# A gated mix of a spectral filter and a dense Mish layer: gate weights as one row, w1 in three other pieces, four tiles transposed by DMA, a narrower last output, and a new order

## The chip, the cores and the metric

The kernel runs on one core of a Trainium2 chip. The metric is the device time of one execution in microseconds. A profile shows one execution: the engines are TensorE (PE in the profile, its weight loads PEld), VectorE (DVE), ScalarE (ACT), GpSimd (POOL) and SyncE (SP). SP and ACT also issue DMAs (SPq and ACTq in the profile).

## The reference

```python
# A_x: 1 x 2048 x 512; w_r, w_i: 2048 x 257; w1: 512 x 1792; w2: 1792 x 512; all bf16
g = sigmoid((x * gate_w).sum(-1, keepdims=True))           # one gate for each of 2048 rows
a = irfft2(rfft2(x) * (w_r + 1j * w_i))                    # spectral filter over rows and columns
h = x @ w1 + b1
b = (h * tanh(softplus(h))) @ w2                           # dense layer with Mish
return g * a + (1 - g) * b
```

Both branches take the same x.

## The kernel before, in words

All 2048 rows are held as 16 tiles of 128 rows (row 16p + t stands on partition p of tile t). Two chains of work share TensorE.

The dense branch: each tile is transposed on TensorE (`tr0` to `tr15`, L544: four 128-wide transposes) and copied from PSUM to `xT` (`evx`, L475). For each of four chunks of 512 rows and each of 14 slices of w1 there is one product `m{chunk}_{slice}` (L788: four 512-wide matmuls) and one Mish activation `h{chunk}_{slice}` on ScalarE (L792). An output tile then is `n{tile}_0` (L815: 14 matmuls, 512 wide).

The spectral branch is a two-dimensional Fourier transform made of small matrix products, each group being four 128-wide matmuls: `p` over the partitions (L567), `d` over the columns (L581, with the constants `FD`, loaded by `cFD`), a shuffle by DMA through SBUF (`sh`), `t` (L666, constants `M`, loaded by `ldM`), the filter on VectorE (`p2`, `p1`, `ad`, L679 to L687, with the weights copied into place by `wrm`, `wim`, `win` and duplicated by the DMAs `wrn`), an edge correction (`e1`, `xp`, `ead`, `e2`, `e3`), and then the way back: `it` (L740), a DMA shuffle `hx`, `id` (L764), `ec` and `ey` on VectorE and ScalarE, and `ip` (L799). Results of `p`, `d`, `t`, `it` are evicted from PSUM 1024 elements wide by `ep`, `ed`, `et`, `eit` (L475) on ScalarE or VectorE.

The gate: `gt` (L589, VectorE, one for each tile) multiplies a tile by the gate weights and sums; `ez`, `ez1`, `omg`, `gc` make g and 1 - g. The gate weights must stand on all 128 partitions (`gwr`); the DMA `gw` reads the one row 128 times. An output tile is scaled and added by `o` and `s` (L804, L805, L809) and leaves by `out` DMAs.

The order is written out by hand as one string (`ORDER`): each token names a task, its engine and its PSUM banks or scratch buffers. Each engine runs its tasks strictly in that order, and the semaphores follow from the data. A wait on one engine therefore holds everything behind it on that engine. A DMA stands in the order of the engine that issues it. The filter products cannot start before all copies of w_r and w_i into place that they need, the activations `h2` wait for the `sh` DMAs and `h3` for all weight copies, because their outputs take over that memory. `warm` and the fillers `fl0`, `fl1`, `fl2` (products with ones, 14 and 3, 8, 5 of them) keep TensorE at work in the beginning. `tab` is a one-element Mish activation at the head of ScalarE's list, which brings the activation table.

Of the kernel before, what the change touches and what calls it, by code (L numbers as in the profile page):

```python
# [306 lines left out]
h0_3:act evx5:act tr6:pe:4 evx6:dve tr4:pe:6 tr7:pe:7 evx7:act cFD:sp evx4:dve
p4:pe:2 p5:pe p6:pe:0 p7:pe h0_5:act ep6:act m1_4:pe:7 m1_3:pe:6 h1_3:act
gt0:dve ep4:dve gt1:dve gt2:dve m1_2:pe:2 gt3:dve h1_2:act h1_4:act bf8_0:dve
bf8_1:dve gt4:dve m0_11:pe:3 h0_11:act m1_8:pe:6 h1_8:act tr11:pe:7 evx11:act m0_7:pe:2  # L310
h0_7:act m1_10:pe:6 h1_10:act bf12_1:dve tr9:pe:7 evx9:dve p8:pe:0 p9:pe ep8:act
m0_9:pe:2 tr8:pe:3 p10:pe:4 bf12_0:dve p11:pe p12:pe:0 p13:pe p14:pe:6 p15:pe
h0_9:act ep10:act ep12:act gt5:dve ep14:dve m1_6:pe:2 h1_6:act m0_10:pe:4 h0_10:act
d6:pe:0 evx8:dve gt6:dve gt7:dve gt8:dve d7:pe tr10:pe:2 d4:pe:6 d5:pe
tr12:pe:3 m1_12:pe:4 evx12:dve ed3:act gt9:dve m0_13:pe:5 ed2:act tr15:pe:3 d2:pe:0
d3:pe h1_12:act h0_13:act ed1:act evx15:dve gt10:dve gt11:dve evx10:act d0:pe:6
d1:pe d14:pe:4 d15:pe m1_11:pe:3 m0_8:pe:0 ed0:act ed7:act m1_0:pe:2 tr14:pe:1
h0_8:act h1_11:act wi0s1:sp wi0s2:sp evx14:act wr0s1:sp wr0s0:sp wr1s1:sp wr1s0:sp
wrm001:dve wrm010:dve gt12:dve gt13:dve gt14:dve wrm100:dve d8:pe:4 d9:pe m0_6:pe:6
m1_9:pe:3 tr13:pe:7 gt15:dve wip0:pool wip1:pool ed4:act h1_0:act h0_6:act evx13:dve  # L320
m0_4:pe:1 d12:pe:4 d13:pe m1_1:pe:2 h0_4:act h1_9:act ed6:act h1_1:act d10:pe:0
d11:pe m1_5:pe:3 ed5:act m1_7:pe:4 wi0s0:sp m2_8:pe:2 m0_12:pe:5 m3_11:pe:0 wi1s1:sp
sh0_3:sp sh0_0:sp wim011:dve sh0_2:sp h1_5:act ldM0:sp wim111:dve wrm000:dve wim100:dve
wrm110:dve wim101:dve zcl:dve sh0_1:sp wim110:dve m3_0:pe:3 wrm011:dve t1_0:pe:6 wrm101:dve
wrm111:act h1_7:act t1_1:pe wim000:dve wim001:dve wim010:dve m3_10:pe:4 et1:act win0:dve
h3_0:act h0_12:act m3_2:pe:1 t0_0:pe:6 t0_1:pe et0:dve wic0:dve win1:dve m3_9:pe:3
m1_13:pe:5 wiz0:dve p20_0:dve:0 p21_0:dve:1 h3_2:act h3_11:act h3_10:act ez:pool ldM1:sp
t3_0:pe:0 t3_1:pe sh1_0:sp sh1_2:sp sh1_3:sp sh1_1:sp h1_13:act et3:act m2_10:pe:4
h2_10:act h2_8:act m2_9:pe:5 h2_9:act h3_9:act m2_12:pe:0 t2_0:pe:6 t2_1:pe m2_6:pe:1
m2_4:pe:3 wrn01:sp wrn00:sp et2:act p20_1:dve p21_1:dve p23_0:dve:2 p23_1:dve h2_4:act  # L330
m3_4:pe:6 ldM3:sp t6_0:pe:4 wrc0:dve wrz0:dve p1_3:dve ez1:dve omg:dve ad_3:dve
p1_1:dve t6_1:pe h2_12:act et6:act p1_0:dve wic1:dve t7_0:pe:2 t7_1:pe m2_7:pe:0
et7:act h2_7:act m2_11:pe:7 ldM2:sp wrn10:sp t5_0:pe:4 wiz1:pool ad_0:dve ad_1:dve
t5_1:pe m2_2:pe:2 h2_2:act et5:act wrn11:sp wrc1:dve m3_3:pe:0 m3_6:pe:3 m2_3:pe:2
t4_0:pe:4 t4_1:pe p27_0:dve:0 wrz1:dve p26_0:dve:1 h3_6:act h3_3:act et4:act m3_7:pe:3
m2_1:pe:0 h2_1:act h2_6:act h2_11:act m3_8:pe:4 m3_12:pe:5 m2_13:pe:1 m3_1:pe:7 p22_0:dve:2
p27_1:dve p22_1:dve p1_7:dve p26_1:dve p1_6:dve ad_7:dve h3_12:act h2_13:act p1_2:dve
p25_0:dve:0 ad_6:dve w2_9:sp w2_4:sp w2_0:sp p24_0:dve:1 n5_0:pe:5 h3_8:act h3_7:act
h3_1:act h3_4:act p25_1:dve p24_1:dve ad_2:dve p1_5:dve ad_5:dve edge:sp ldG0:sp
p1_4:dve ad_4:dve o5_0:dve n6_0:pe:3 o6_0:act h2_3:act e1:pe:5 gc:dve xp20:dve:0  # L340
xp21:dve xp1:dve:1 rft:sp ldG3:sp ead:dve:2 m2_5:pe:6 m2_0:pe:7 h2_5:act h2_0:act
inv:sp ldG1:sp e2:pe:2 m3_13:pe:3 e3:dve ldG2:sp it1_0:pe:0 it1_1:pe eit1:dve
it5_0:pe:4 it5_1:pe h3_13:act eit5:act m3_5:pe:7 h3_5:act it2_0:pe:2 it2_1:pe it7_0:pe:0
eit2:act it3_0:pe:4 it3_1:pe it7_1:pe eit7:act eit3:act n4_0:pe:7 it0_0:pe:0 it4_0:pe:2
it0_1:pe it6_0:pe:4 it6_1:pe it4_1:pe eit6:act eit4:act eit0:dve hx8_0:act hx4_1:act
hx8_1:act o4_0:act hx0_0:act n0_0:pe:6 n2_0:pe:2 n3_0:pe:7 id10:pe:0 id11:pe id8:pe:4
hx4_0:act ec10:dve:0 ey10_1:dve ey10_0:dve id9:pe ec8:act:1 hx12_0:act o2_0:act o0_0:act
ey8_0:dve ey8_1:dve n1_0:pe:3 id6:pe:0 ip9:pe:6 o1_0:act o9:act id4:pe:4 ip10:pe:2
id5:pe id7:pe ec6:act:0 ip8:pe:3 ip11:pe:6 hx0_1:sp hx12_1:sp o3_0:dve o11:dve
ec4:act:1 o8:act n7_0:pe:7 ey6_1:dve ey6_0:dve o10:act ip6:pe:6 ip7:pe:0 ey4_0:dve  # L350
id2:pe:2 ey4_1:dve ip4:pe:1 id0:pe:4 id1:pe id3:pe ec0:act:0 o7_0:act s6:dve
ec2:act:1 s4:dve ey0_0:dve n11_0:pe:6 ey0_1:dve s7:dve ey2_1:dve id12:pe:0 ip0:pe:7
ip5:pe:4 id13:pe n10_0:pe:5 s11_0:dve s5:dve s0:dve ey2_0:dve ip3:pe:4 id14:pe:2
id15:pe ip1:pe:7 ec12:act:0 out5:act out7:act ec14:act:1 ey12_1:dve ey12_0:dve ip12:pe:6
ip2:pe:0 n8_0:pe:1 s1:dve ey14_0:dve ey14_1:dve ip13:pe:7 ip15:pe:2 n9_0:pe:3 s3:dve
s8_0:dve s10_0:dve ip14:pe:1 out11:sp out1:sp s2:dve o12:dve n12_0:pe:6 s12_0:dve
n13_0:pe:0 o13:dve s13_0:dve s9_0:dve o14:dve out13:act o15:act out3:act out9:sp
n15_256:pe:7 n14_0:pe:6 s14_0:dve out14:act s15_256:dve out15_256:sp n15_0:pe:1 s15_0:dve out15_0:act
"""


def _build(nc, A_x, A_w_r, A_w_i, B_x, B_w1, B_b1, B_w2, gate_w, out, XTP=16, LATE=8, NWARM=14,
           W1P=((0, 2), (2, 6), (6, 14)), XP=((0, 2), (2, 4), (4, 8), (8, 12), (12, 16)), SH=2):
# [7 lines left out]
    G = _Graph()  # L371
    es = ExitStack()
    with es:
# [100 lines left out]
        def evac(name, o, i, n, reads, writes, cls, engs=("act", "dve"), deps=()):  # L474
            fns = dict(dve=lambda e: e.tensor_copy(out=o(), in_=i()), act=lambda e: e.activation(o(), i(), AF.Copy))  # L475
# [410 lines left out]
```

## Time and profile before

| | us |
|---|---|
| runs | 135.01, 133.9, 134.84 (median 134.84) |
| the profiled execution: its time | 134.83 |
| its span, from the first instruction to the last | 133.2 |
| TensorE busy | 127.2 (95%) |
| VectorE busy | 87.9 (66%) |
| ScalarE busy | 77.4 (58%) |
| GpSimd busy | 5.4 (4%) |

The granted TensorE clock is 1.0 throughout. A row such as "80.36 3.02 PE ps L815 x14" of the chain of waits says: from 80.36 us on, 3.02 us of the chain are 14 instructions of line 815 on TensorE that write `ps`. In a row of the groups stand the line, engine, operation, output and inputs, shapes and count, then busy time and the mean of one in ns, then the idle time ahead of them and what ended it. In the rows of the DMA issues the last number is the time from issue to landing in us.

### The profile page before, as it was taken

How to read it: one execution, taken by the hardware profiler on the slowest of the kernel's cores; microseconds unless marked ns; L12 is line 12 of the kernel's file. 1: busy time of each engine (PE TensorE's matmuls, PEld its weight loads, DVE VectorE, ACT ScalarE, POOL GpSimd, SP SyncE). 2: the span in 40 equal slices, each digit the busy share in tenths (PEclk: the TensorE clock that was granted, in tenths of full speed). 3: DMA queues.
4: the chain of work that ended last, by engine and by line, in shares of the span. 5: the costliest groups of instructions: out<-in, count | busy, mean ns of one | idle time of the engine just before them, and what ended most of it. 6: DMA issues, size and time to landing. Idle time of an engine off the chain costs nothing.

```text
span 133.2 us, 2246 instructions
## 1 busy us (share of the span) xinstructions
PE 127.2 (95%) x901; PEld 71.5 (54%) x901; DVE 87.9 (66%) x162; ACT 77.4 (58%) x110; POOL 5.4 (4%) x13
## 2 busy tenths in 40 slices
...
GB/s 100 145 351 407 307 205 170 172 56 0 245 270 199 219 229 238 220 259 359 348 316 1 0 0 5 0 241 310 74 9 0 0 58 99 0 162 0 0 236 79
DMA packets 12533, 20.28 MB, mean 152 GB/s; under 512 B 1324, under 2 KB 6956, under 8 KB 12460
## 3 DMA queue, kind: packets, MB, share of 16 engines
...
q8 instruction: 7, 0.11, 0.4%
q14 instruction: 2, 0.02, 0.0%
...
## 4 chain that ended last, share of the span: by engine, by line
PE 58%; DVE 30%; DMA 6%; issue 4%; SPq 1%; DVEq 0%
PE ps L815 32%; PE ps L788 14%; DVE tmp L679 7%; DMA w_sb<-in_B_w_dram 6%; DVE rC L684 4%; DVE rC L687 4%; PE ps L740 3%; PE ps L764 3%; PE ps L799 3%; PE ps L567 2%; DVE w_sb L589 2%; DVE rW L630 2%; DVE rA L630 2%; DVE rA L640 2%; PE ps L544 2%
## 5 line engine op out<-in xcount | busy, mean ns | idle before, releaser
L788 PE MATMUL ps<-rX,w_sb 128*128 128x512 bf16 x224 | 51.9, 379 | 1.7 <-DMA w_sb<-in_B_w_dram 1.7
L788 PEld LDWEIGHTS ps<-rX,w_sb 128*128 128x128 bf16 x224 | 20.8, 98 | 23.3 <-issue 1.9
L815 PE MATMUL ps<-w_sb,hs 128*128 128x512 bf16 x112 | 25.0, 379 | 0.0
L792 ACT ACTIVATE hs<-ps,b1f 128x512 bf16<-128x512 f32 x28 | 18.5, 696 | 3.4 <-PE ps L788 3.2
L815 PEld LDWEIGHTS ps<-w_sb,hs 128*128 128x128 bf16 x112 | 10.8, 98 | 12.4
L475 ACT ACTIVATE rC<-ps 128x1024 bf16<-128x1024 f32 x13 | 13.2, 1031 | 1.2 <-PE ps L567 0.7
L815 PE MATMUL ps<-w_sb,rD 128*128 128x512 bf16 x56 | 12.7, 379 | 0.0
L557 DVE TENSOR_TENSOR rB<-rA 128x1024 bf16<-128x1024 bf16 (+1 forms) x10 | 5.5, 580 | 11.0 <-DMA rA<-in_A_x_dram 11.0
L815 PE MATMUL ps<-w_sb,rS 128*128 128x512 bf16 (+1 forms) x70 | 12.3, 336 | 0.0
L809 DVE SCALAR_TENSOR_TENSOR rX<-ps,omg,rX 128x512 bf16<-128x512 f32 (+1 forms) x9 | 5.9, 689 | 9.3 <-PE ps L815 9.3
L475 ACT ACTIVATE tmp<-ps 128x512 f32<-128x512 f32 x7 | 4.1, 597 | 13.4 <-PE ps L764 13.3
L589 DVE SCALAR_TENSOR_TENSOR w_sb<-rA,w_sb 128x512 bf16<-128x512 bf16 x16 | 11.0, 687 | 0.3
L792 ACT ACTIVATE rD<-ps,b1f 128x512 bf16<-128x512 f32 x14 | 9.1, 698 | 3.1 <-PE ps L788 3.1
L679 DVE TENSOR_TENSOR tmp<-rC,rA 64x1024 bf16<-64x1024 bf16 x16 | 10.6, 686 | 0.4
L804 ACT ACTIVATE rX<-ps,gcol 128x512 bf16<-128x512 f32 x4 | 2.6, 690 | 14.0 <-DVE rX L809 14.0
L774 DVE TENSOR_TENSOR rA<-tmp,ps 128x512 bf16<-128x512 f32 x16 | 10.0, 679 | 0.4 <-ACT tmp L475 0.4
L815 PEld LDWEIGHTS ps<-w_sb,rS 128*128 128x128 bf16 x70 | 6.8, 98 | 5.5
L792 ACT ACTIVATE rS<-ps,b1f 128x512 bf16<-128x512 f32 x14 | 9.0, 696 | 0.7 <-PE ps L788 0.3
L815 PEld LDWEIGHTS ps<-w_sb,rD 128*128 128x128 bf16 x56 | 5.4, 98 | 6.1
L804 ACT ACTIVATE rX<-ps,omg 128x512 bf16<-128x512 f32 x6 | 4.0, 685 | 7.4 <-PE ps L815 5.1
L475 ACT ACTIVATE rD<-ps 128x1024 bf16<-128x1024 f32 x8 | 8.0, 1035 | 0.0
L475 ACT ACTIVATE rF<-ps 128x1024 bf16<-128x1024 f32 x6 | 5.8, 1029 | 2.2 <-PE ps L740 2.2
...
## 6 DMA issues: line engine op xcount, KB each, us to landing
rE<-rD SPq DMA_DIRECT2D x8, 256.0 KB, 3.6
...
rC<-rF ACTq DMA_DIRECT2D x6, 256.0 KB, 3.4
w_sb<-in_B_w_dram SPq DMA_DIRECT2D x2, 640.0 KB, 11.4
...
```

The source lines that it names most:

```text
L475: fns = dict(dve=lambda e: e.tensor_copy(out=o(), in_=i()), act=lambda e: e.activation(o(), i(), AF.Copy))
L557: return e.tensor_tensor(out=xu[:, a:b_, uv, :], in0=x_sb[:, a:b_, 0:256], in1=x_sb[:, a:b_, 256:512], op=ALU.add if uv == 0 else ALU.subt ...
L589: t_gt.append(dve(f"gt{t}", "gate", "stt", 512, lambda e, t=t: e.scalar_tensor_tensor(out=junk, in0=x_sb[:, t, :], scalar=1.0, in1=gwr, op ...
L630: return e.tensor_copy(out=o_, in_=i_)
L679: return e.tensor_tensor(out=zv(z)[lo], in0=Y[hi, f0:f0 + 8, :], in1=Wi[hi, f0:f0 + 8, 0:128], op=ALU.mult)
L684: return e.tensor_tensor(out=Y[:, f0:f0 + 8, :], in0=Y[:, f0:f0 + 8, :], in1=Wr[:, f0:f0 + 8, 0:128], op=ALU.mult)
L774: return e.tensor_tensor(out=yb[:, t:t + 2, 256 * h:256 * h + 256].rearrange("p t (i e) -> p t i e", e=2), in0=t4(z), in1=o4(bank(b, 1)), ...
L788: ins = e.matmul(bank(b), w1_sb[:, dt_, 128 * ft:128 * (ft + 1)], xT[:, c, dt_, :, :], start=(dt_ == 0), stop=(dt_ == 3))
L792: G.add(f"h{c}_{ft}", "mish", dict(act=lambda e, c=c, ft=ft, b=b: e.activation(hs[c][:, ft, :], bank(b), AF.Mish, bias=b1f[:, ft:ft + 1])) ...
L804: f_a = lambda e: e.activation(o_()[0], o_()[1], AF.Copy, scale=o_()[2])
L809: dve(name, "fin", "psums", hi - lo, lambda e: e.scalar_tensor_tensor(out=bs[:, t, lo:hi], in0=bank(b)[:, 0:hi - lo], scalar=col[:, t:t + ...
L815: ins = e.matmul(bank(b)[:, 0:hi - lo], hs[c][:, ft, 128 * tl:128 * (tl + 1)], w2_sb[:, ft, lo:hi], start=(ft == 0), stop=(ft == NFT - 1))
```

## The change

Five edits and a new order:

- The gate weights come as one row of 1 KB (`gwl`, into a free row of SBUF). A product with a row of ones (`gwb`) spreads it over 128 partitions into PSUM, and `gwe` copies it to `gwr`. The 128 KB broadcast `gw` goes.
- w1 comes in pieces of 4, 5 and 5 slices of 128 columns, where it came in pieces of 2, 4 and 8.
- Tiles 12 to 15 are no longer transposed on TensorE; four DMA transposes (`xt12` to `xt15`, on SP) read x again from memory and write `xT`.
- The last output tile is made in 384 and 128 columns, where it was 256 and 256.
- Of the fillers only `fl0` stays.
- The order of all engines is written anew. Among other things: `x8` and `w1_9` are issued by ACT; `tab` moves from the head of ScalarE's list to a place behind `h3_13`; the wide evictions go to other engines (VectorE has `ep2`, `ep6`, `ep10`, `ep14`, `ed0`, `ed6`, `et5`, `et0`, `et1` up to `e1`, where it had `ep4`, `ep14`, `et0`); the filter weights' copy `wrm101` goes to ScalarE; `n2` and `n1` stand ahead of `e1` and `n5` behind it, where `n5` and `n6` stood ahead; all of m but `m2_0` stands ahead of `e1`.

```diff
-FILL = (3, 8, 5, )
+FILL = (3, )
 ORDER = """
-warm:pe:0 wrp0:pool ebase:pool ones:pool wrp1:pool ident:pool cRF:act braw:act x0:sp
-fl0:pe:1 tr0:pe:0 x2:sp w1_0:sp w1_2:sp bf0_0:dve bf0_1:dve bf2_1:dve x4:sp
-tr1:pe:1 gw:act tab:act bf2_0:dve evx1:dve fl1:pe:2 tr2:pe:2 evx0:act tr3:pe:3
-evx2:act tr_b:pe:0 p0:pe:4 p1:pe p2:pe:6 ep0:act evx3:dve ev_b:dve fl2:pe:2
-m0_1:pe:0 m0_0:pe:1 p3:pe w1_6:sp x8:sp x12:sp h0_1:act wi1s0:act wr0s2:sp
...
-n15_256:pe:7 n14_0:pe:6 s14_0:dve out14:act s15_256:dve out15_256:sp n15_0:pe:1 s15_0:dve out15_0:act
+cRF:act wrp1:pool ones:pool ident:pool braw:act x0:sp warm:pe:0 fl0:pe:1 tr0:pe:0
+tr1:pe:1 gwl:act x2:sp w1_0:sp x4:sp x8:act x12:sp w1_4:sp wr0s0:sp
+wi0s2:sp cFD:sp bf0_0:dve bf0_1:dve tr2:pe:2 tr3:pe:3 tr_b:pe:4 gwb:pe:5 w1_9:act
+wr0s2:act evx0:dve bf2_1:dve bf2_0:dve evx1:act p2:pe:0 p3:pe p0:pe:6 p1:pe
+evx2:act evx3:dve ep0:act wr0s1:act m0_1:pe:3 m0_2:pe:2 gwe:dve gt0:dve gt1:dve
+ev_b:dve ep2:dve tr7:pe:4 tr6:pe:5 m0_3:pe:6 tr5:pe:7 h0_2:act h0_1:act evx7:act
+tr4:pe:3 bf4_1:dve bf4_0:dve p6:pe:0 tr8:pe:2 m0_0:pe:4 p7:pe ldM0:act evx6:act
...
+p15:pe evx9:act ep12:act h0_5:act m1_0:pe:0 m0_4:pe:6 h1_0:act h0_4:act ep14:dve
+d14:pe:2 d15:pe d10:pe:0 d0:pe:4 d1:pe ed7:act gt2:dve ed0:dve gt3:dve
...
+m1_11:pe:4 t2_1:pe h1_11:act p23_0:dve:2 p21_1:dve xt13:sp xt14:sp xt12:sp xt15:sp
+m3_0:pe:6 p23_1:dve m3_9:pe:5 m1_13:pe:4 m0_6:pe:2 m3_11:pe:3 wrm111:act h3_9:act et2:act
...
+m3_7:pe:2 tab:act et6:act h3_8:act h1_13:act wrc1:dve p25_0:dve:1 p27_0:dve:0 m2_6:pe:6
...
+p26_0:dve:1 ad_4:dve p27_1:dve p1_7:dve ad_7:dve p26_1:dve p1_6:dve ad_6:dve omg:dve
+o2_0:act o1_0:dve e1:pe:6 xp20:dve:0 xp1:dve:1 xp21:dve ead:dve:2 n5_0:pe:3 o5_0:act
...
+s9_0:dve s8_0:dve out9:sp out13:sp s10_0:dve out11:sp s7:dve out7:act n15_0:pe:6
+s15_0:dve out15_0:act n15_384:pe:5 s15_384:dve out15_384:act
 """
-def _build(..., XTP=16, LATE=8, NWARM=14, W1P=((0, 2), (2, 6), (6, 14)), ...):
+def _build(..., XTP=12, LATE=8, NWARM=14, W1P=((0, 4), (4, 9), (9, 14)), ...):
...
-        dma("gw", gwr, gate_w.unsqueeze(0).to_broadcast([128, 512]), kb=128, writes=["gw"])
+        dma("gwl", junk[0:1, :], gate_w.unsqueeze(0), kb=1, writes=["gwl", "junk"])
...
         for t in range(XTP, NT):
             dma(f"xt{t}", xT[:, t // 4, :, t % 4, :], xv[:, t, :], queue=("sp",), transpose=True, kb=128, writes=[("xT", t)])

+        gb = _Buf("b1")
+        G.add("gwb", "small", dict(pe=lambda e: e.matmul(bank(gb), one[0:1, :], junk[0:1, :], start=True, stop=True)), ("pe", 1, 512), reads=["gwl"], writes=[gb])
+        evac("gwe", lambda: gwr, lambda: bank(gb), 512, [gb], ["gw"], "small")
...
-                for lo, hi in ([(0, 256), (256, 512)] if t == NT - 1 else [(0, 512)]):
+                for lo, hi in ([(0, 384), (384, 512)] if t == NT - 1 else [(0, 512)]):
                     b2 = _Buf("b1")
-                    keys = [("bs", t, h) for h in (0, 1) if lo <= 256 * h < hi]
+                    keys = bsk if t < NT - 1 else bsk[:1] if lo == 0 else bsk[1:]
```

More of the change, by code (lines that the diff above doesn't have):

```diff
@@ L307 @@
[L307 to L356, printed above, removed]
@@ new lines @@
+wi0s2:sp cFD:sp bf0_0:dve bf0_1:dve tr2:pe:2 tr3:pe:3 tr_b:pe:4 gwb:pe:5 w1_9:act
[3 more added lines that the diff above has]
+tr4:pe:3 bf4_1:dve bf4_0:dve p6:pe:0 tr8:pe:2 m0_0:pe:4 p7:pe ldM0:act evx6:act
+h0_3:act ldM2:act h0_0:act wi1s0:act evx4:dve evx5:dve bf8_0:dve evx8:dve bf8_1:dve
+ep6:dve m1_1:pe:5 h1_1:act m1_3:pe:2 h1_3:act p10:pe:6 p11:pe tr11:pe:4 p4:pe:0
@@ new lines @@
+p5:pe ep4:act p8:pe:2 m1_4:pe:5 h1_4:act p9:pe ep8:act bf12_1:dve ep10:dve
+tr9:pe:0 m0_5:pe:1 tr10:pe:5 bf12_0:dve p12:pe:6 p13:pe p14:pe:2 evx10:dve evx11:dve
+p15:pe evx9:act ep12:act h0_5:act m1_0:pe:0 m0_4:pe:6 h1_0:act h0_4:act ep14:dve
+d14:pe:2 d15:pe d10:pe:0 d0:pe:4 d1:pe ed7:act gt2:dve ed0:dve gt3:dve
+d11:pe m2_13:pe:6 wi1s1:act ed5:act d12:pe:2 d13:pe d8:pe:4 m1_6:pe:7 h1_6:act
+ed6:dve gt4:dve gt5:dve d9:pe ed4:act sh1_3:act m0_11:pe:0 m0_9:pe:7 d6:pe:2
+d7:pe ed3:act gt6:dve gt7:dve gt8:dve d4:pe:4 d5:pe m1_5:pe:1 m0_7:pe:2
@@ new lines @@
+m0_8:pe:3 ed2:act h0_11:act h0_8:act gt9:dve wrm000:dve gt10:dve gt11:dve gt12:dve
+gt13:dve h0_7:act m2_12:pe:0 gt14:dve gt15:dve wim101:dve zcl:dve wim100:dve sh1_2:sp
+wi0s0:sp d2:pe:4 wi0s1:sp wim010:dve wim011:dve wrm010:dve wrm001:dve wrm011:dve sh1_0:act
+sh1_1:act wip0:pool h0_9:act wim001:dve d3:pe ed1:act sh0_3:sp m1_8:pe:3 m1_7:pe:2
+m1_12:pe:7 m0_10:pe:4 h1_8:act h1_5:act h0_10:act sh0_2:sp sh0_1:sp h1_12:act m1_10:pe:3
+m1_9:pe:1 h1_7:act h1_9:act h1_10:act m2_2:pe:7 m1_2:pe:2 m0_13:pe:3 h0_13:act h1_2:act
@@ new lines @@
+sh0_0:sp h2_12:act h2_13:act m2_8:pe:1 h2_8:act t5_0:pe:4 t5_1:pe m2_1:pe:3 m2_7:pe:2
+et5:dve wim000:dve h2_1:act h2_7:act h2_2:act t4_0:pe:4 t1_0:pe:0 t4_1:pe m0_12:pe:6
+h0_12:act win0:dve wic0:dve t0_0:pe:2 t0_1:pe et4:act wr1s0:sp ldM1:sp wr1s1:sp
+t1_1:pe m2_5:pe:7 m2_9:pe:6 wrm101:act et0:dve t3_0:pe:2 m2_4:pe:4 h2_4:act h2_9:act
+wip1:pool wrp0:pool wiz0:pool t3_1:pe m2_10:pe:5 et3:act h2_10:act p20_0:dve:0 wim110:dve
+et1:dve wim111:dve p20_1:dve win1:dve wic1:dve wrm100:dve p21_0:dve:1 wrm110:dve t2_0:pe:0
@@ new lines @@
+m1_11:pe:4 t2_1:pe h1_11:act p23_0:dve:2 p21_1:dve xt13:sp xt14:sp xt12:sp xt15:sp
+m3_0:pe:6 p23_1:dve m3_9:pe:5 m1_13:pe:4 m0_6:pe:2 m3_11:pe:3 wrm111:act h3_9:act et2:act
+h3_11:act h0_6:act wrn01:sp wrn00:sp wrc0:dve wrz0:dve p1_3:dve ad_3:dve p1_0:dve
+ad_0:dve p1_1:dve ebase:pool ldM3:sp wrn10:sp wrn11:sp wiz1:pool ez:pool m3_12:pe:5
+w2_9:sp w2_0:sp h2_5:act w2_4:act m2_11:pe:0 t7_0:pe:2 t7_1:pe m3_3:pe:7 et7:act
+h2_11:act h3_0:act h3_3:act m3_13:pe:1 m3_5:pe:2 m3_8:pe:0 m2_3:pe:3 t6_0:pe:6 t6_1:pe
```

26 lines of the change are left out of this document (22 added, 4 removed).

## The prediction

> **What bounds the kernel now.** I read the page's busy rows first, then the chain of waits, then busy time by stretch.
>
> ```profile
> span 133.2 us, 2246 instructions
> PE 127.2 (95%) x901; PEld 71.5 (54%) x901; DVE 87.9 (66%) x162; ACT 77.4 (58%) x110; POOL 5.4 (4%) x13
> ```
>
> ```profile
> 1.71 7.49 DMA w_sb<-in_B_w_dram
> 9.33 1.89 PE ps L788 x8
> ...
> 14.03 0.89 PE ps L544 x16
> ...
> 30.28 0.42 DVE rX L475
> ...
> 73.41 0.67 DVE rX L805
> ...
> 78.16 0.86 PE ps L788 x4
> ...
> 80.36 3.02 PE ps L815 x14
> ...
> 118.95 12.14 PE ps L815 x70
> 131.11 0.48 DVE rX L809
> ```
>
> ```profile
> core 0: us, PE busy (x) PEld busy (x) DVE busy (x) ACT busy (x) POOL busy (x), PEclk, DMA share, GB/s
> 4.10:9.33 5.23, 2.90 (x45) 2.44 (x43) 2.26 (x7) 2.22 (x3) 0.00 (x0) 1.00 0.73 234
> 9.33:26.80 17.47, 17.47 (x141) 10.35 (x142) 11.38 (x25) 14.96 (x22) 0.00 (x0) 1.00 1.08 257
> 26.80:50.70 23.90, 23.90 (x191) 13.99 (x190) 22.38 (x46) 23.04 (x33) 0.48 (x2) 1.00 0.58 176
> 50.70:74.10 23.40, 22.69 (x135) 11.30 (x133) 22.56 (x41) 17.14 (x27) 3.59 (x2) 1.00 0.83 241
> ```
>
> The chain has three parts. Until 9.33 TensorE waits for the first piece of w1. From there to 131.1 it has no gap that counts but one, just before 74.1. Between 30.3 and 73.4, though, the chain runs over VectorE, which is busy for 44.9 of 47.3 us (22.38 + 22.56): there TensorE is only just covered by filler products. Last come 0.48 us of the final output and its DMA. So there are four places where time can go: the start, TensorE's work, VectorE's work up to the edge correction e1, and the tail.
>
> I call the start of the first w1 product T0 (9.33 now). Unit prices from the chain: one m (four 512-wide products) 0.86, one n 3.02, a group of four 128-wide products (tr, p, d, t, it, id) 0.89/4 = 0.222.
>
> **The change part by part.**
>
> *The start: gate row, w1 pieces, fillers.*
>
> ```profile
> 1.71 0.98 SPq L463 DMA_DIRECT2D w_sb<-in_B_w_dram  x2
> 1.97 0.37 ACTq L463 DMA_DIRECT2D w_sb<-in_gate_w_dram  x1
> 2.37 1.28 ACT L505 ACT_TABLE_LOAD   x1 [2.37 <-issue]
> 3.66 0.20 ACT L505 ACTIVATE omg<-const-float32-1.0 128x1 f32<-128x1 f32 x1
> 7.15 0.45 PE L498 MATMUL ps<-const-bfloat16-1.0 128*128 128x128 bf16 x5
> 9.33 1.89 PE L788 MATMUL ps<-rX,w_sb 128*128 128x512 bf16 x8 [1.73 <-DMA w_sb<-in_B_w_dram]
> 10.39 0.69 ACT L792 ACTIVATE hs<-ps,b1f 128x512 bf16<-128x512 f32 x1 [2.24 <-PE ps L788]
> ```
>
> ```profile
> w_sb<-in_gate_w_dram ACTq DMA_DIRECT2D x1, 128.0 KB, 6.8
> DMA to landing us min/median/max: 6.8/7.5/8.5
> ```
>
> The last row is the answer for the issues around 2.2 us, three of them: the gate weights (6.8), w1's first 256 KB (7.5, the 7.49 of the chain) and w1's 512 KB, the second of the two SP issues, at about 2.2 (8.5, so 10.7). The gate broadcast takes 6.8 us for 128 KB, from 1.97 to 8.8, exactly while w1's first piece is late. It goes, but the first piece grows to 512 KB, and x8 now comes over ACT's queue close behind. Best case: T0 falls to 7.6, where TensorE's own front work ends (7.15 + 0.45): -1.7. Worst case: it lands when 512 KB lands now, 10.7: +1.4. I take half of the wait, -0.9, because the broadcast's 6.8 is so far out of line for its size. The removed fillers and the one product with ones sit inside this wait and cost nothing. If that cover is gone, the product costs one 512-wide pass, 0.86/4 = 0.22.
>
> *The first Mish activation ("tab") moves from ahead of evx0 to far behind.* Then evx1, a plain copy, is ScalarE's first activation, and a table load has to come again ahead of h0_2. That is 1.28 us. Either ScalarE's idle time there (2.24 now) hides it, or it sits behind the wait for m0_2. Then h0_2 and h0_1 are late, and behind them tr4, which needs h0_1's bank: TensorE has only 0.86 + 3 x 0.22 = 1.5 us of work in between, against 1.4 us for the two activations. Bounds 0 and +1.3; I take the middle, +0.6. Ahead of it evx1 can be late by another load, inside the wait for w1.
>
> The Trainium skill ("ScalarE: Activation LUTs", What ACT_TABLE_LOAD costs) adds a drain of about 1.38 us to a load of 1.28. The rows above speak against it: the load ends at 3.65 and the activation starts at 3.66. By that rule the sum below would be 1.4 us higher.
>
> *TensorE's work behind T0.* Four transposed tiles go (-4 x 0.222), and all of p0 to p3 now stands ahead of T0 (one group, -0.222): -1.1. The order's sum from T0 falls from 120.3 to 119.2; now it takes 131.1 - 9.33 = 121.8.
>
> *VectorE up to e1.*
>
> ```profile
> L475 DVE CAST rC<-ps 128x1024 bf16<-128x1024 f32 x3 | 3.7, 1222 | 0.9 <-PE ps L567 0.9
> L475 DVE COPY rX<-ps 128x512 bf16<-128x512 bf16 x9 | 3.6, 417 | 1.7 <-PE ps L544 1.7
> L589 DVE SCALAR_TENSOR_TENSOR w_sb<-rA,w_sb 128x512 bf16<-128x512 bf16 x16 | 11.0, 687 | 0.3
> L589 DVE DVE_READ_ACCUMULATOR w_sb<-rA,w_sb 128x1 f32 x16 | 1.3, 81 | 0.0
> L630 DVE COPY rW<-rS 32x2064 bf16<-32x2064 bf16 x4 | 2.8, 696 | 0.1
> L640 DVE TENSOR_SCALAR rA<-rA 64x4160 bf16<-64x4160 bf16 x2 | 2.5, 1237 | 0.1
> L679 DVE TENSOR_TENSOR tmp<-rC,rA 64x1024 bf16<-64x1024 bf16 x16 | 10.6, 686 | 0.4
> PE ps L699 <- DVE rX L805: 0.7, 1, 0.7
> ```
>
> The new order gives VectorE nine wide evictions (ep2, ep6, ep10, ep14, ed0, ed6, et5, et0, et1) where it had three: +6 x 1.22. It adds gwe (nearest rows 0.42 and 1.22 for half and double the work; about 0.7) and takes away two tile evictions (-0.83) and one weight copy (-0.7): +6.5. VectorE has room before 26.8 (13.6 busy of 22.7 us), so what counts is what stands behind ep14. TensorE reaches the end of p15 at T0 + 8 x 0.86 + 8 x 0.222 + 12 x 0.222 = T0 + 11.4, and ep14 ends at T0 + 12.6. From gt2 to ad_6 the list is 14 gt (0.77), five evictions (1.22), 14 copies (0.70), two win (1.24), 32 filter operations (0.686) and 1.7 of small ones: 52.8. It waits some 0.8 before ed0, since d1 ends only at T0 + 14.2. So the filter ends at T0 + 66.2. TensorE reaches e1 at T0 + 55 x 0.863 + 52 x 0.222 + 2 x 3.02 = T0 + 65.1. That leaves a wait of about 1.1 against 0.7 now: +0.4. Bounds: -0.7 (no wait) and +2.6, if VectorE is again busy for only 95% of the stretch.
>
> *The constants FD.*
>
> ```profile
> 26.95 0.45 PE ps L581 x8
> w_sb<-c_front SPq DMA_DIRECT2D x1, 128.0 KB, 15.5
> 7.49 0.57 SPq L463 DMA_DIRECT2D w_sb<-c_front  x1
> ```
>
> FD lands at 7.5 + 15.5 = 23.0 now, for d6 at 26.95. The first d (d14) moves up to T0 + 13.1, about 22. The bytes queued ahead of it are much the same, x and w1, now with wr0s0. Bounds 0 and +2 (24, if the loads of w_r and w_i beside it take more); I take +0.3. All six d groups queue behind that wait.
>
> *Transposes by DMA.* No row shows one. SP issues them behind sh0_0 and three loads, at about T0 + 30, and m3_0 needs them at T0 + 41.7: 10 us. The nearest rows: 256 KB from SBUF to SBUF land in 3.6 us each, and the broadcast's 128 KB in 6.8. Together or overlapped that is hidden (0); four in a row at 3.6 are 14.4, +4. I take 0.
>
> ```profile
> rE<-rD SPq DMA_DIRECT2D x8, 256.0 KB, 3.6
> out_dram<-rX SPq DMA_DIRECT2D x1, 64.0 KB, 1.6
> L809 DVE SCALAR_TENSOR_TENSOR rX<-ps,omg,rX 128x512 bf16<-128x512 f32 x7 | 5.1, 748 | 8.9 <-PE ps L815 8.9
> L809 DVE SCALAR_TENSOR_TENSOR rX<-ps,omg,rX 128x256 bf16<-128x256 f32 x2 | 1.0, 480 | 0.4 <-PE ps L815 0.4
> ```
>
> *The tail.* From 512 to 256 columns the last operation falls by 0.27, so 128 columns take about 0.35: -0.13. The 384-wide one (0.61) hides behind 14 products of 0.056 (0.78). The DMA stays near 1.6. Together -0.15.
>
> Sum: -0.9 + 0.6 - 1.1 + 0.4 + 0.3 - 0.15 = -0.85. The span goes from 133.2 to 132.35. The profiled execution took 134.83, 1.6 more than its span and equal to the median of the runs (134.84), so I predict 134.0 us.
>
> **The rivals.**
>
> *The start pays in full.* w1 lands by 7.6 and ScalarE's idle time hides the table load: another -0.8 and -0.6, 132.6. For it: 2.24 us idle at that place, and the odd 6.8 of the broadcast. Against it: twice the bytes.
>
> *VectorE sets e1 (the other side).* Behind ep14 VectorE has no slack. With the share of now (95%) its 52.8 become 55.4 and e1 waits 2.6 longer: 136.6. It decides from the point where VectorE loses over 1 us to waits between ed0 and ad_6. For it: it is the chain from 30 to 73 already, and gets six evictions more. Against it: the loads before 26.8 have room.
>
> *The change doesn't relieve the start.* w1's larger piece lands at 10.7 as 512 KB do now: +1.4 in place of -0.9, 136.3. For it: the 8.5 us row. Against it: the broadcast no longer runs beside it.
>
> *The transposes are late.* In series, +4: 138.0. Everything on TensorE behind m3_0 stands, and SP's wrn loads behind the four with it. Against it: 10 us of room. The Trainium skill ("Advanced Engine Details and Errata", X-Bar Transpose (TRN2)) calls such transposes as fast as regular DMAs, which would keep them hidden; no row here shows one.
>
> **How the numbers follow.** The forecast gets 0.36, the start in full 0.22, VectorE 0.16, no relief 0.14, the transposes 0.12. One per cent (1.35 us) is about what a measurement here can tell from no change. Faster by more (under 133.5): 0.22 and 0.10 of the forecast, 0.32. Slower by more (over 136.2): 0.11 of VectorE, 0.07 of no relief, 0.09 of late transposes and 0.02 of the forecast, 0.29. Between: 0.39. The range 132.2 to 137.2 takes in the start, VectorE and no relief and leaves most of the late transposes out.
>
> **What would show it.** T0 between 8 and 9; a second table load ahead of h0_2 and whether tr4 waits behind it; no wait at d14; e1 waiting about 1 us for VectorE; no wait at m3_0. The prediction is wrong if T0 is over 10, if m3_0 waits for a DMA, or if TensorE needs over 122 us from T0 to its end.

## The result and the profile after

The changed kernel takes 138.87 us (median of four runs, 137.67 to 139.33), the kernel before 134.44 beside it: a ratio of 1.0315, 95% interval 1.0232 to 1.0399. It is slower; 134.0 was predicted, with a range up to 137.2. The profiled execution took 138.94. Medians are of all executions, and ratios leave out those that lie far above a kernel's fastest.

The page of the changed kernel, its first rows and the row of the granted clock in 40 slices of 3.4 us:

```profile
span 137.7 us, 2188 instructions
...
PE 129.6 (94%) x873; PEld 70.6 (51%) x873; DVE 97.4 (71%) x166; ACT 72.0 (52%) x102; POOL 5.4 (4%) x15
...
PEclk9985699999999999999999999999999999999999
```

TensorE executes 28 products fewer than before and is busy for 2.4 us longer. The clock row says why: from the third to the fifth slice the full clock was not granted. Before, the row held only nines. The timeline of TensorE at that place (start, duration, operation, and in brackets the idle time ahead with what ended it):

```profile
6.83 0.83 PE L570 MATMUL ps<-w_sb,rB 128*128 128x128 bf16 x12
11.32 3.57 PE L791 MATMUL ps<-rX,w_sb 128*128 128x512 bf16 x8 [3.65 <-DMA w_sb<-in_B_w_dram]
14.69 1.06 PE L547 MATMUL ps<-identt,rA 128*128 128x128 bf16 x8
15.54 1.38 PE L791 MATMUL ps<-rX,w_sb 128*128 128x512 bf16 x4
16.76 0.61 PE L547 MATMUL ps<-identt,rA 128*128 128x128 bf16 x8
```

T0 is 11.32, 2.0 later than the 9.33 of before. And the eight products behind it take 3.57 us where the same eight took 1.89. From 11.32 to 16.76 stand three m and two tr, by the prediction's prices 3 x 0.86 + 2 x 0.222 = 3.0 us of work; they take 5.44. So the clock costs 2.4 more. Busy time by stretch, with the granted clock as the column behind POOL:

```profile
11.32:16.85 5.53, 5.53 (x22) 2.56 (x23) 1.29 (x2) 1.92 (x4) 0.00 (x0) 0.55 1.10 268
16.85:30.00 13.15, 13.15 (x143) 9.20 (x142) 10.20 (x18) 10.64 (x15) 0.00 (x0) 1.00 0.52 130
```

The transfers issued in the first 30 us (KB each, us from issue to landing):

```profile
w_sb<-in_B_w_dram ACTq DMA_DIRECT2D x1, 640.0 KB, 12.7
...
w_sb<-in_B_w_dram SPq DMA_DIRECT2D x1, 512.0 KB, 9.5
rA<-in_A_x_dram ACTq DMA_DIRECT2D x1, 512.0 KB, 7.6
...
w_sb<-c_front SPq DMA_DIRECT2D x1, 128.0 KB, 15.0
```

w1's first 512 KB land 9.5 us after their issue at 1.72: at 11.2. Beside them run x8 and the last 640 KB of w1, both on ACT's queue. FD lands at 6.88 + 15.0 = 21.9, ahead of the first d at 26.8. The other places that the prediction named, from the waits, SP's timeline and the end of the timeline:

```profile
PE ps L702 <- DVE rC L690: 1.1, 1, 1.1
```

```profile
43.76 6.59 SPq L462 DMA_TRANSPOSE rX<-in_A_x_dram  x4
```

```profile
135.03 0.62 DVE L812 SCALAR_TENSOR_TENSOR rX<-ps,omg,rX 128x384 bf16<-128x384 f32 x1 [1.08 <-PE ps L818]
...
135.81 0.35 DVE L812 SCALAR_TENSOR_TENSOR rX<-ps,omg,rX 128x128 bf16<-128x128 f32 x1 [0.17 <-PE ps L818]
```

The edge product waits 1.1 us for VectorE, m3_0 waits for nothing, and the span ends 1.9 us behind 135.81 (2.1 before). The difference of 4.5 us in the span is then: start +2.0, clock +2.4, the rest from T0 to the last product +0.3 (135.81 - 11.32 - 2.4 = 122.1 against 121.8), tail -0.2.

### The profile page after: what moved, and what is told of

Same layout as the page of the kernel before. It is cut to its first block, busy times and chain, and to the rows that moved or that the text cites. A ratio compares the mean times of both kernels' runs of the same rounds, so it can differ in the third digit from the quotient of the medians.

```text
span 137.7 us, 2188 instructions
## 1 busy us (share of the span) xinstructions
PE 129.6 (94%) x873; PEld 70.6 (51%) x873; DVE 97.4 (71%) x166; ACT 72.0 (52%) x102; POOL 5.4 (4%) x15
## 4 chain that ended last, share of the span: by engine, by line
PE 75%; DVE 11%; DMA 7%; ACT 4%; issue 1%; SPq 1%; DVEq 0%
PE ps L818 31%; PE ps L791 28%; DMA w_sb<-in_B_w_dram 7%; DVE tmp L682 3%; PE ps L743 3%; ACT rS L795 3%; PE ps L767 3%; PE ps L584 3%; PE ps L802 3%; PE ps L669 2%; PE ps L570 2%; DVE rC L475 2%; PE ps L547 2%; DVE rC L690 2%; DVE rA L634 1%
## 5 line engine op out<-in xcount | busy, mean ns | idle before, releaser
L791 PE MATMUL ps<-rX,w_sb 128*128 128x512 bf16 x224 | 54.2, 390 | 3.7 <-DMA w_sb<-in_B_w_dram 3.7
L818 PEld LDWEIGHTS ps<-w_sb,hs 128*128 128x128 bf16 x112 | 10.9, 98 | 12.5 <-DVE rX L808 0.2
L807 ACT ACTIVATE rX<-ps,omg 128x512 bf16<-128x512 f32 x7 | 4.7, 685 | 18.6 <-PE ps L818 12.6
L818 PE MATMUL ps<-w_sb,rS 128*128 128x512 bf16 (+2 forms) x70 | 12.8, 336 | 0.0
L475 ACT ACTIVATE rC<-ps 128x1024 bf16<-128x1024 f32 x9 | 9.2, 1020 | 1.6 <-PE ps L570 1.2
L812 DVE SCALAR_TENSOR_TENSOR rX<-ps,gcol,rX 128x512 bf16<-128x512 f32 x8 | 5.7, 744 | 5.8 <-PE ps L802 5.8
L475 DVE COPY tmp<-ps 128x512 f32<-128x512 f32 x5 | 3.4, 689 | 9.0 <-PE ps L767 8.9
L807 ACT ACTIVATE rX<-ps,gcol 128x512 bf16<-128x512 f32 x6 | 3.9, 684 | 10.8 <-PE ps L802 10.8
L818 PEld LDWEIGHTS ps<-w_sb,rS 128*128 128x128 bf16 x70 | 6.3, 98 | 5.7
L812 DVE SCALAR_TENSOR_TENSOR rX<-ps,omg,rX 128x512 bf16<-128x512 f32 (+2 forms) x9 | 6.1, 688 | 4.3 <-PE ps L818 4.3
L475 DVE CAST rC<-ps 128x1024 bf16<-128x1024 f32 x7 | 8.5, 1221 | 0.7 <-PE ps L669 0.5
```

The costliest lines, as they stand in the source:

```text
L791: ins = e.matmul(bank(b), w1_sb[:, dt_, 128 * ft:128 * (ft + 1)], xT[:, c, dt_, :, :], start=(dt_ == 0), stop=(dt_ == 3))
L807: f_a = lambda e: e.activation(o_()[0], o_()[1], AF.Copy, scale=o_()[2])
L812: dve(name, "fin", "psums", hi - lo, lambda e: e.scalar_tensor_tensor(out=bs[:, t, lo:hi], in0=bank(b)[:, 0:hi - lo], scalar=col[:, t:t + ...
L818: ins = e.matmul(bank(b)[:, 0:hi - lo], hs[c][:, ft, 128 * tl:128 * (tl + 1)], w2_sb[:, ft, lo:hi], start=(ft == 0), stop=(ft == NFT - 1))
```

## The experiments

Theory: two loads on ACT's queue make w1's first piece late, and the idle TensorE then loses its clock. Rivals: the larger first piece of w1 alone; the removed broadcast and fillers; the order of the work behind T0. Each run is named by its whole label; in the expectations, e2 or e5 stands for the run that begins so, and e1 without more for the edge product. Ratios are to the kernel before on the same chip.

**Filling the idle time.** 48 products of 128 columns ahead of m0_1:

```diff
-FILL = (3, )
+FILL = (3, 48, )
- m0_1:pe:3 m0_2:pe:2
+ fl1:pe:3 m0_1:pe:3 m0_2:pe:2
```

> The changed kernel with 48 more products with ones (128 wide) on TensorE directly ahead of the first w1 product, in the time in which it waits for w1 (7.7 to 11.3 us). Theory (idle TensorE loses its clock): the granted clock stays at full speed behind 11.3, the first two m take 1.7 us and not 3.6, the start of the first w1 product stays at 11.3, and the span falls by about 2.6 us, to 135.1. Rival (the half-speed stretch has another cause, such as DMA traffic into SBUF): the products behind 11.3 stay at 0.43 us each and the span stays at 137.7.

Measured: 135.84 us, ratio 1.0166 (1.0104 to 1.0228), clock 1.0 in all runs. TensorE's timeline:

```profile
7.52 2.98 PE L498 MATMUL ps<-const-bfloat16-1.0 128*128 128x128 bf16 x48
10.85 1.67 PE L791 MATMUL ps<-rX,w_sb 128*128 128x512 bf16 x7 [0.35 <-DMA w_sb<-in_B_w_dram]
```

About half of the loss goes, with w1 still late. The order behind m0_1 is the same, the idle time is filled, and the clock stays full: the half clock came from the idle time. Where the first row of m shows x7 and not x8, here and below, the record of one product is missing; the weight loads put the first product at 10.6 here, and, at full clock, some 0.25 ahead of the row in the others.

**Off ACT's queue.** x8 and w1_9 on SP:

```diff
- x4:sp x8:act x12:sp w1_4:sp wr0s0:sp
+ x4:sp x8:sp x12:sp w1_4:sp w1_9:sp wr0s0:sp
- gwb:pe:5 w1_9:act
+ gwb:pe:5
```

> The changed kernel with x8 and the last piece of w1 issued by SP, behind x4 and behind w1_4, and not by ACT. Theory (w1's first piece is late because x8 on the second queue is interleaved with it): the first w1 product starts at 7.6 to 8.5, TensorE has no idle time there, the clock stays full, and the span falls by 4 to 5.5 us to 132 to 134. Rival (the piece is late because it has 512 KB): the first product still starts above 10.5 and the clock falls as before.

Measured: 137.59 us, ratio 1.028 (1.0207 to 1.0353). Transfers, then TensorE:

```profile
w_sb<-in_B_w_dram SPq DMA_DIRECT2D x1, 512.0 KB, 5.0
```

```profile
7.42 1.67 PE L791 MATMUL ps<-rX,w_sb 128*128 128x512 bf16 x7
...
11.35 0.40 PE L547 MATMUL ps<-identt,rA 128*128 128x128 bf16 x4 [0.72 <-ACT hs L795]
...
24.43 2.66 PE L584 MATMUL ps<-w_sb,rC 128*128 128x128 bf16 x24 [3.06 <-DMA w_sb<-c_front]
```

The same 512 KB land in 5.0 us instead of 9.5, and T0 is 7.42 with no wait: the two loads together explain the late start. The time hardly falls, since the stall moved. FD now stands behind x8 and w1_9 as well on SP (512 and 640 KB), the first d waits 3.06 us for it, and the clock falls again behind that wait (24 products in 2.66 us, in the changed kernel 1.50). The second table load, hidden in the changed kernel, now holds tr4 for 0.72.

**A smaller first piece.** w1_0 in two loads:

```diff
-W1P=((0, 4), (4, 9), (9, 14))
+W1P=((0, 2), (2, 4), (4, 9), (9, 14))
- x2:sp w1_0:sp x4:sp
+ x2:sp w1_0:sp w1_2:sp x4:sp
```

> The changed kernel with w1's first piece of four slices split into two of two slices (two DMAs of 256 KB one after the other on SP). Theory of the second queue: the first 256 KB still meet x8 on the way; the first product starts at 9 to 10.5, the second some later, and the clock falls or not by the length of the wait. Theory of the size: the first product starts at about 7.7 to 9.3, since half the bytes are needed, and the span falls by 2 to 4 us.

Measured: 137.42 us, ratio 1.0192 (1.0106 to 1.0278). TensorE in the profiled run of 136.02:

```profile
7.58 0.81 PE L791 MATMUL ps<-rX,w_sb 128*128 128x512 bf16 x3
10.63 1.04 PE L791 MATMUL ps<-rX,w_sb 128*128 128x512 bf16 x4 [2.24 <-DMA w_sb<-in_B_w_dram]
```

In this execution the numbers come close to the expectation of the size (7.58, and a span of 134.8, 2.9 less), while that of the second queue failed for the first half. But the second half is nearly as late as the whole piece was, so a smaller piece splits the wait, and e2_after_sp shows that the 512 KB need not be late. The four runs took 136.02, 136.55, 138.29 and 139.06 us at granted clocks of 1.0, 0.987, 0.988 and 0.975. Only the first was traced: its gap of 2.24 us did not cost the clock. The other three lost it, and how long their gaps were is not known.

**The broadcast back in.** The gate weights by the 128 KB broadcast again, without the product and its eviction:

```diff
-dma("gwl", junk[0:1, :], gate_w.unsqueeze(0), kb=1, ...)
+dma("gw", gwr, gate_w.unsqueeze(0).to_broadcast([128, 512]), kb=128, ...)
...
```

> The changed kernel with the gate weights broadcast by DMA again (128 KB on ACT's queue, no row, no product with ones, no copy). If the broadcast is what made w1 late in the kernel before, w1's first piece comes still later, the first product at 12.5 to 14, and the span grows by 1 to 3 us. If it was harmless, the first product stays at 11.3 within 0.5 and the span within 0.7 us of 137.7.

Measured: 137.94 us (134.81 to 139.59), too far spread for a ratio. In the profiled run, at 137.73 us with a span of 136.4, the landing of w1's first piece and TensorE:

```profile
w_sb<-in_B_w_dram SPq DMA_DIRECT2D x1, 512.0 KB, 9.1
```

```profile
5.12 0.62 PE L544 MATMUL ps<-identt,rA 128*128 128x128 bf16 x8 [0.55 <-DMA rA<-in_A_x_dram]
...
7.16 1.86 PE L567 MATMUL ps<-w_sb,rB 128*128 128x128 bf16 x16 [1.30 <-ACT rX L475]
11.31 2.99 PE L788 MATMUL ps<-rX,w_sb 128*128 128x512 bf16 x7 [2.29 <-DVE rC L475]
```

The piece lands 9.1 us after its issue with the broadcast and 9.5 without, and the first product starts at 10.9 by the weight loads. So the removal of the broadcast bought nothing in the changed kernel. This trace also lost the clock sooner than the others: TensorE waits 0.55 us for x and 1.30 for a copy on ScalarE, with 0.7 us of work between, and from 7.14 on the granted clock is half for 6.83 us. The 16 products of p take 1.86 us at it, 1.05 in the changed kernel.

**FD ahead of the last w1.** As e2_after_sp, with cFD issued between w1_4 and w1_9:

```diff
- w1_4:sp w1_9:sp wr0s0:sp wi0s2:sp cFD:sp
+ w1_4:sp cFD:sp w1_9:sp wr0s0:sp wi0s2:sp
```

> The changed kernel with x8, x12, w1_4, FD and w1_9 all on SP's queue in this order, so that FD is issued ahead of the last 640 KB of w1. If the wait for FD (3.06 us at the first d) and the half clock behind it are what was left of e2's 136.9 us of span: T0 at 7.4, no wait of a d for FD, granted clock 1.0, span 131.5 to 132.5, ratio to the kernel before 0.985 to 1.0. If the changed order of the work costs time in itself (its waits on VectorE and ScalarE ahead of e1): span 134 to 136 though TensorE waits for no transfer, ratio 1.00 to 1.02.

Measured: 133.75 us, ratio 0.9987 (0.9948 to 1.0026); profiled span 132.6 (up to 132.5 was expected), clock 1.0.

```profile
7.14 1.89 PE L791 MATMUL ps<-rX,w_sb 128*128 128x512 bf16 x8 [0.16 <-DMA w_sb<-in_B_w_dram]
...
23.07 1.02 PE L791 MATMUL ps<-rX,w_sb 128*128 128x512 bf16 x4 [0.75 <-DMA w_sb<-in_B_w_dram]
```

The loss is gone. No d waits for FD, but w1_9 is now the late one, by 0.75.

**Mish's table early.** As e5_after_sp_fd, and:

```diff
- gwl:act x2:sp
+ gwl:act tab:act x2:sp
- m3_7:pe:2 tab:act et6:act
+ m3_7:pe:2 et6:act
```

> As e5, with the activation that loads Mish's table moved from late in ScalarE's queue to its head, behind the early transfers it issues. If the second table load is now exposed (tr4 waited 0.72 us for the first Mish in e2): one table load in the trace, ahead of the first eviction, and 0.5 to 0.8 us less than e5. If it is hidden or moved to the first eviction instead: within 0.3 us of e5.

Measured: 134.31 us, ratio 0.9974 (0.9939 to 1.001). The profiled run, at 137.17 us, shows the danger that was left:

```profile
24.73 1.11 PE L791 MATMUL ps<-rX,w_sb 128*128 128x512 bf16 x4 [2.73 <-DMA w_sb<-in_B_w_dram]
```

```profile
25.40:28.80 3.40, 3.40 (x20) 2.12 (x19) 2.03 (x4) 0.00 (x0) 0.00 (x0) 0.52 0.02 5
```

w1_9 comes 2.73 us late, and the clock is half for the next 3.4 us. The trace has one table load, at 2.24, and tr4 no longer waits for the first Mish (0.27 in e5_after_sp_fd). The gain in time is 0.1% and within the interval; this run doesn't decide it.

**The row and the fillers in the kernel before.** One run with the row, the product `gwb` and its eviction in place of the broadcast; one without fl1 and fl2:

```diff
- gw:act tab:act
+ gwl:act tab:act
- ev_b:dve fl2:pe:2
+ ev_b:dve gwb:pe:2 gwe:dve fl2:pe:2
...
```

```diff
-FILL = (3, 8, 5, )
+FILL = (3, )
```

> The kernel before with only the gate weights changed: one row of 1 KB by DMA, a product with ones, an eviction on VectorE. By the forecast's term for the start: first w1 product earlier than 9.33, by 0.5 to 1.7 us, ratio 0.985 to 0.995. If the broadcast never held up w1 (128 KB of 3.5 MB moved in the first 15 us): first w1 product at 9.3 within 0.3, ratio 0.997 to 1.004.

> The kernel before without its second and third group of fillers (8 and 5 products of 128 columns), which the change removes too. If the granted clock falls only when TensorE has been idle for about 3.4 us in one piece: its idle time ahead of the first w1 product grows from 1.73 to at most 2.6 us, the clock stays at 1.0, ratio 0.997 to 1.004. If shorter idle times are enough, or if the fillers stood in several gaps at once: the clock falls for 3.4 or 6.8 us and the ratio is 1.01 to 1.02.

Measured: 1.0028 (0.9996 to 1.006) and 1.0033 (0.9992 to 1.0074), both nothing that can be told from no change. The first w1 product, with the row and without the fillers:

```profile
8.06 1.89 PE L791 MATMUL ps<-rX,w_sb 128*128 128x512 bf16 x8
```

```profile
7.92 1.89 PE L788 MATMUL ps<-rX,w_sb 128*128 128x512 bf16 x8 [0.86 <-ACT rC L475]
```

Both are earlier than 9.33, and these two executions are shorter by as much: spans of 131.9 and 131.8 against 133.2. The medians are no better all the same, so 9.33 was itself one draw, and a late one. The median span of the kernel before was 132.0 to 132.3 on the four later chips, and with the same start of the order T0 was 8.47 and 9.43 in e10_before_xt and e11_before_xt_tail below. With the row w1's first 256 KB landed 5.3 us after their issue, with the broadcast after 6.1 to 7.5 in four kernels; one execution doesn't tell whether that is the broadcast. And once w1 is early, the first product waits for an eviction instead (0.86 here), so less was to be had at the start than the 1.73 us of the profile.

**All queues of the changed kernel mended.** As e6_after_sp_fd_tab, with the two 512 KB loads of c_m off ACT's queue, behind all of w1:

```diff
- p7:pe ldM0:act evx6:act h0_3:act ldM2:act h0_0:act
+ p7:pe evx6:act h0_3:act h0_0:act
- wi0s2:sp bf0_0:dve
+ wi0s2:sp ldM0:sp ldM2:sp bf0_0:dve
```

> The changed kernel with all its queue choices mended: x8, w1_9 and FD as in e5, Mish's table loaded at the head of ScalarE's queue as in e6, and the two early 512 KB loads (ldM0, ldM2), which in e5 and e6 were issued on ACT's queue at 9.4 and 10.5 us and shared the engines with w1_9, issued on SP behind all of w1. If those loads held up w1_9: no wait of 0.75 to 2.7 us at 21 to 24 us, granted clock 1.0 in every run, T0 at 7.2, span 131.0 to 131.8, median 132.3 to 133.1, ratio 0.985 to 0.995. If w1_9 is late because all of the first 3.9 MB needs until 23 us at the engines' rate: the wait stays at 0.5 us or more and the ratio within 0.995 to 1.005.

Measured: 132.93 us, ratio 0.9933 (0.9909 to 0.9958), clock 1.0 in all eleven runs.

```profile
7.04 1.67 PE L791 MATMUL ps<-rX,w_sb 128*128 128x512 bf16 x7
9.11 0.62 PE L547 MATMUL ps<-identt,rA 128*128 128x128 bf16 x8 [0.40 <-DMA rA<-in_A_x_dram]
```

```profile
129.48 0.35 DVE L812 SCALAR_TENSOR_TENSOR rX<-ps,omg,rX 128x128 bf16<-128x128 f32 x1 [0.16 <-PE ps L818]
```

No piece of w1 holds TensorE up any more, as the first expectation said. Only queues and the place of one activation differ from the changed kernel, and 5.9 us lie between them (138.87 against 132.93, on two chips whose kernels before took 134.44 and 133.76). So the loss lay in the queues, not in what the change computes. But e9_after_queues gains at its start alone: from its first product (6.8 by the weight loads) to the last output operation it takes 122.7 us, where the kernel before took 121.8 and e10_before_xt, next, 120.8 (129.06 less 8.25, by the weight loads there). The new order of the work behind T0 costs time in itself.

**The parts that worked, in the kernel before.** XTP=12 with the four transposes on SP behind `wr1s0:sp`; then the last output in 384 and 128 columns as well:

```diff
-XTP=16
+XTP=12
...
- wr0s1:sp wr0s0:sp wr1s1:sp wr1s0:sp
+ wr0s1:sp wr0s0:sp wr1s1:sp wr1s0:sp xt12:sp xt13:sp xt14:sp xt15:sp
```

> The kernel before with only its last four tiles of x transposed by DMA, issued on SP behind the last weight load, where SP is idle from 20.5 to 33.2 us. By the forecast (16 matmuls of 56 ns less on TensorE, nothing waits for the transposes): 0.9 us less, ratio 0.992 to 0.995, no wait of m3_0 for a DMA. If the transposes' small packets hold up other transfers or SP's queue (the shuffles that start at 33.2): a wait ahead of the t stage and a ratio of 1.00 or above.

> The kernel before with the two parts of the change that worked in the changed kernel's trace: the DMA transposes as in e10 and the last output in 384 and 128 columns. By the forecast's terms: 0.15 to 0.2 us below e10, ratio 0.990 to 0.994, span's end 1.9 us behind the end of TensorE's work instead of 2.1. If the shorter last piece saves nothing (its 14 products of 128 columns cost what its shorter eviction and transfer save): within 0.1 us of e10.

Measured: 132.63 us, 0.9917 (0.9884 to 0.995), and 132.42 us, 0.9901 (0.9869 to 0.9934). SP, the last output operation and the start in the first, then the start in the second:

```profile
16.24 10.88 SPq L462 DMA_TRANSPOSE rX<-in_A_x_dram  x4
```

```profile
129.06 0.48 DVE L809 SCALAR_TENSOR_TENSOR rX<-ps,omg,rX 128x256 bf16<-128x256 f32 x1 [0.39 <-PE ps L815]
```

```profile
8.47 1.67 PE L788 MATMUL ps<-rX,w_sb 128*128 128x512 bf16 x7 [0.83 <-DMA w_sb<-in_B_w_dram]
```

```profile
9.43 1.67 PE L788 MATMUL ps<-rX,w_sb 128*128 128x512 bf16 x7 [1.80 <-DMA w_sb<-in_B_w_dram]
```

The transposes give 1.1 us (0.83%, by the interval 0.5 to 1.2%), as 16 products of 56 ns (0.9) should. One of the twelve executions of the first took 190.85 us at a granted clock of 0.661, which no trace explains. The tail's 0.2 us lies in the expected direction and inside both intervals. Both kernels are faster than the kernel before, and e9_after_queues can't be told from them.

**One load on ACT's queue, in the kernel before.** x8 moved there:

```diff
- w1_6:sp x8:sp x12:sp
+ w1_6:sp x12:sp
- gw:act tab:act
+ gw:act x8:act tab:act
```

> The kernel before with one edit: the 512 KB load of x8 issued on ACT's queue, behind the gate's broadcast and ahead of the table load, instead of on SP behind all of w1. If a second queue that moves large tiles beside SP's is what made w1's first piece late in the changed kernel: the first w1 product starts 1 to 2.5 us later than in e8 and e7 (7.9 and 8.1), span 133 to 134.5, ratio 1.007 to 1.02. If the lateness came from the larger first piece of w1 itself (512 KB rather than 256): the first w1 product at 8 to 9.3 as before and a ratio of 0.997 to 1.003.

Measured: ratio 1.0058 (1.0026 to 1.009). Neither expectation held whole:

```profile
7.53 1.67 PE L788 MATMUL ps<-rX,w_sb 128*128 128x512 bf16 x7 [0.74 <-DMA w_sb<-in_B_w_dram]
...
10.52 2.75 PE L788 MATMUL ps<-rX,w_sb 128*128 128x512 bf16 x12 [1.09 <-ACT rC L475]
```

In this execution the first 256 KB were not late, nor the 512 KB behind them (8.2 us after their issue, 7.2 to 8.5 in the four kernels without x8 on ACT's queue); the kernel lost a little elsewhere. So one load on the second queue need not delay a small first piece. Three of its ten executions took 137.3 to 137.5 us at a granted clock of 0.987, and none of the 28 of the kernel before beside them lost the clock. No trace shows what was late in those three. Which of the two loads delays 512 KB was left open, too.

**One of the two loads at a time, in the changed kernel.** Only x8 back on SP, or only w1_9:

```diff
- x4:sp x8:act x12:sp
+ x4:sp x8:sp x12:sp
```

```diff
- w1_4:sp wr0s0:sp ... w1_9:act
+ w1_4:sp w1_9:sp wr0s0:sp
```

> The changed kernel with one edit: x8 on SP behind x4, while w1_9 (640 KB) stays on ACT's queue, where it is then issued at about 2.2 us. If any large load on the second queue makes w1's first piece late: T0 at 9.5 to 11.5 as in the changed kernel, its landing 7.5 us or more after its issue, granted clock below 1.0. If it is x8 alone, or both together that do it: T0 at 7.0 to 8.0, landing within 6 us.

> The changed kernel with one edit: w1_9 on SP behind w1_4, while x8 (512 KB) stays on ACT's queue. If any large load on the second queue is enough, or x8 alone: T0 at 9.5 to 11.5, landing of w1's first piece 7.5 us or more after its issue, granted clock below 1.0. If both are needed: T0 at 7.0 to 8.5.

Measured: 135.37 us, 1.0113 (1.0062 to 1.0165), and 136.03 us, 1.0163 (1.0086 to 1.0239). For each the landing of w1's first 512 KB and T0, x8 moved first:

```profile
w_sb<-in_B_w_dram SPq DMA_DIRECT2D x1, 512.0 KB, 5.6
```

```profile
7.46 1.89 PE L791 MATMUL ps<-rX,w_sb 128*128 128x512 bf16 x8 [0.26 <-DMA w_sb<-in_B_w_dram]
```

```profile
w_sb<-in_B_w_dram SPq DMA_DIRECT2D x1, 512.0 KB, 7.7
```

```profile
9.54 2.44 PE L791 MATMUL ps<-rX,w_sb 128*128 128x512 bf16 x8 [2.41 <-DVE rC L475]
```

With both loads on ACT's queue the piece landed 8.8, 9.1 and 9.5 us after its issue in three kernels, with neither 4.7 to 5.3 in four: that difference is far above the spread. With x8 alone T0 is 9.54, with w1_9 alone 7.46, with both 11.32. So x8 is the load that counts more; what w1_9 adds to it, some 1 to 2 us, rests on one traced execution of each of these two kernels. In the last row the trace names VectorE as the releaser. The same product starts at 7.04 in e9_after_queues, where that eviction ends at 9.45, so it doesn't wait for it; w1 lands at 1.72 + 7.7 = 9.4. Both runs are still slower than before, because FD and w1_4 were late in the one (waits of 0.61 and 1.25 us) and T0 in the other.

## Why the prediction was wrong

*The start, the step that failed first.* The prediction took -0.9, half of the wait, with +1.4 as its worst; it measured +2.0. It blamed the broadcast for the late first piece, and treated x8 "over ACT's queue close behind" as a remark without a price. The worst case took the landing of 512 KB from a kernel whose ACT queue was empty behind the broadcast. e2_after_sp, e13_after_x8_sp and e14_after_w19_sp give the price: 5.0 and 5.6 us for the piece without x8 beside it, 7.7 with x8, and the changed kernel 9.5 with both. The 9.33 that the term started from was a late draw as well. The Trainium skill ("DMA: Bandwidth & Descriptors", Queues, rings and completion order) says that each DMA engine takes turns between its queues, packet by packet; an early load on one queue then shares with a later one on the other. The landings agree. The prediction did not draw on it.

*"The removed fillers ... sit inside this wait and cost nothing."* This was the second failure, +2.4 us. In the kernel before that was nearly so: without them e8_before_nofill took 1.0033 (0.9992 to 1.0074), with a wait of 0.86 in its trace. In a wait of 3.65 us the idle time itself cost the clock. The prediction named the hidden work, and not what keeps the clock granted. The 13 removed products would have filled only 13 x 0.056 = 0.7 us of that wait; no run shows whether they would have saved the clock there. The 48 of e1_after_fill, 3.0 us of work, did. The Trainium skill ("TensorE: Matmul & The Clock Gate", HAM oscillation — how this bites in real kernels) has the rule: no idle time of TensorE over about 3.4 us. By it the changed kernel's 3.65 us should halve the clock, and it did; 2.41, 2.73 and 3.06 us were enough in three traces here, and two shorter waits in e4_after_bcast, so the rule is too generous. The rival "no relief of the start" had the place, and lacked both the queue and the clock: 136.3 against 138.9. The rival nearest in number, the late transposes (138.0), had no part in it: m3_0 waited for nothing.

*The table load, +0.6 (0 to 1.3).* It cost 0 in the changed kernel, hidden in the late start (9.02 to 10.30, ahead of T0). The mechanism was right: with T0 at 7.42 in e2_after_sp, tr4 waited 0.72 us behind it. There the load ends at 10.01 and the first Mish starts at 10.03, so the further 1.4 us that the prediction weighed by the rule on the drain did not come.

*TensorE's work, VectorE, FD, transposes, tail.* Behind T0 the prediction's steps sum to 121.8 - 1.1 + 0.6 + 0.4 + 0.3 = 122.0; the trace has 122.1 without the clock. That agreement is luck: the table and FD cost nothing, which leaves 121.1, and 1.0 us went where the prediction had no term. By the starts of its products TensorE loses up to 0.4 us at a time, together some 0.9 between 48 and 63 us and 0.4 at 87 to 89, where the kernel before loses some 0.2 in this way. The longest such place:

```profile
55.75 6.47 PE L791 MATMUL ps<-rX,w_sb 128*128 128x512 bf16 x28
62.43 0.61 PE L669 MATMUL ps<-rE,rF 128*128 128x128 bf16 x8 [0.21 <-ACT hs L795]
```

By the prediction's price 28 products are 28 x 0.86/4 = 6.0 us, and the next starts 6.7 behind the first of them. For the last 0.21 the trace names Mish on ScalarE; the cause of the rest is open. The edge product waited 1.1 us, as forecast, but TensorE and VectorE both reached it 1.1 us later than forecast: it started at 81.03, which is T0 + 67.3 without the clock, and 66.2 was forecast. FD held nothing up, the transposes landed in 5.0 to 7.2 us and stayed hidden, and the tail fell by 0.2 for a forecast 0.15. e10_before_xt shows the -0.9 of the transposes as a measured gain. What the prediction named as signs of being wrong came true in two places: T0 over 10, and over 122 us from T0 to the end (124.5).
